# Squares from rows read back in the expert stage, one routing for three batches, the gate chain in the second phase, six banks for the first transposes

## The chip, the cores and the metric

The kernel runs on one NeuronCore of a Trainium2 chip. The metric is device time in microseconds, the median of several executions. The engines are TensorE (PE in the profile; PEld is its weight load), VectorE (DVE), ScalarE (ACT), GpSimd (POOL) and SyncE (SP, which here only issues DMAs). Each engine works through its own queue in order; an instruction that waits for another engine holds everything behind it on its own queue.

## What is computed

Causal attention with a decay per position, then a mixture of experts in which each token goes to its one best expert, then a dense layer with a maximum over three products.

```python
def _moe_ref(x, expert_emb, tau, w1, w2):
    xn = x / (np.linalg.norm(x, axis=-1, keepdims=True) + 1e-06)
    en = expert_emb / (np.linalg.norm(expert_emb, axis=-1, keepdims=True) + 1e-06)
    logits = xn @ en.T / tau
    expert_idx = np.argmax(logits, axis=1)
    probs = softmax(logits)
    gate_w = probs[np.arange(N), expert_idx]
    for e in range(E):
        mask = expert_idx == e
        out[mask] = gate_w[mask, None] * (np.maximum(x[mask] @ w1[e], 0.0) @ w2[e])

def reference(...):
    x = attention(q, k, v, f)            # 4 batches, 8 heads, 576 positions, 64 wide
    x = x as 2304 rows of 512
    x = _moe_ref(x, ...)                 # 8 experts, 512 -> 1024 -> 512
    h = max(x @ w1, x @ w2, x @ w3)      # 512 -> 768
    return h @ w_out                     # 768 -> 512
```

The norm of a row of x is not needed to choose the expert, only for the gate. The gate scales whole rows, and all products in between allow a positive scale to be pulled out, so the kernel multiplies by it once, at the very end.

## The kernel before

**Three parts.** `attention` (from L215) works through 4 batches x 8 heads, two heads (a pair) at a time. `moe` (from L911) first runs the eight experts, largest first, with a fixed capacity (`CAP`, 384 down to 256 tokens), and then the dense layer over six chunks of 384 tokens; I call these the expert stage and the second phase. Matrix products of weights are done as three matmuls, high x high, high x low, low x high (`mm3`, L906 to L908).

**Order.** Nothing is scheduled by hand. In both parts every step is a task for a small planner (`Sched`, L122 to L205) that runs while the program is built. A task has an engine or a choice of two, a cost in us, a due time (`prio`), tasks it depends on, and a buffer that it takes (`get`) or frees (`rel`). The planner always takes the task that can start first on its own clock, and among equals the one with the smallest due time, and emits it. So costs and due times fix the order of each engine's queue; on the chip the queues then run with semaphores. A `chain` is a generator whose steps are tasks that follow one another.

**Attention.** For each head: scores in pieces (`s`, L344, PE), the row minimum with the mask (L361, DVE), exp (L381, ACT), transposes (L393 to L401, PE), copies of these (L433 on DVE, L435 on ACT). For each pair, in two halves: `po` (L459, PE), a copy `ot`, `pb` (L478, PE; it turns the result back and appends its product with the expert rows), and a scaling into `XL` (L487, DVE). `po` and `pb` share two PSUM banks, `ps_o` (tag "o"). Splits of q and k into high and low part are casts on ACT or DVE (`evict`, L431 to L435) and subtractions on GpSimd (L321, L324). The rows of x go to DRAM (`x_dram`, L498) from SP's queue.

**At the end of a batch** (`batch_out`, L502) two chains start: `route_batch` (L567) finds the expert of each token of the batch's five blocks, its rank within the expert (PE sums over one-hot matrices), and adds the token numbers to a table (`route_table`, L680); `square_sums` (L699) takes five ACT squares with a running sum for the norms. The last batch goes through `first_slot` (L626), which finds the tokens of the largest expert at once. Chains of successive batches follow one another.

**Hand-over.** `sort_experts` (L735) puts the experts in order. `tokens` (L1054) gathers the rows of an expert's tokens in up to three groups (GpSimd, L1065), transposes each (PE, L1072, into an "o" bank) and splits it into high and low part (L934, L1083).

**Expert stage.** `expert_piece` loads a quarter of a weight matrix (SP, `stg`, three buffers), splits it (L934 and L951) into one of four `ring` slots. `ph` is x times w1, `py` h times w2; both use six PSUM banks (tag "y"). `Y` holds the results of all experts side by side; its part past the first expert is cleared by ACT (`clear`, L1103), since experts overlap there. `shared_piece` decodes the weights of the dense layer, which come as float64, with five DVE steps for each half (L1005 to L1020): eight of the twelve during the expert stage, the other four (the last of `w`, three of `w_out`) after the last expert's weights.

**side_work** (L880) computes the gates (`gates`, L795, with a square root and an exponential on ACT) and the table of output rows (`scatter_table`, L834, with PE sums of four times five matmuls), which gives `sidx` and `sgate`. It is queued with due time 30, after `sort_experts`.

**Second phase.** For each chunk: a split of Y (`ysplit`, L1199), 18 groups `pm` of twelve matmuls with the maximum on DVE (L1240), a split of the result (`g`), and three `po` (L1266 to L1268). ACT scales each `po` by `sgate` (`oo`, L1272) and GpSimd scatters it to the output (L1275).

Of the kernel before, what the change touches and what calls it, by code (L numbers as in the profile page):

```python
# [6 lines left out]
F32 = mybir.dt.float32  # L7
# [14 lines left out]
NBLK = 5  # L22
# [10 lines left out]
NCH = 3  # L33
# [181 lines left out]
def attention(tc, g, qT, kT, v, x_dram, es):  # L215
# [308 lines left out]
def routing_consts(nc, g, cp):  # L524
# [33 lines left out]
    g.ss = cp.tile([128, NTB], F32, name="ss")  # L558
    g.oh = cp.tile([128, NTB, E], F16, name="oh")
# [7 lines left out]
def route_batch(nc, g, b, lg, rp, ps):  # L567
    s0 = NBLK * b
    sl = slice(s0, s0 + NBLK)
    SH, SC = [128, NBLK, E], [128, NBLK, NCH]  # L570
    last = b == B - 1
    step = dict(eng="DVE", cost=0.24)
    yield dict(eng="DVE", cost=0.45)
    L = g.L[:, sl, :]
    nc.vector.tensor_reduce(out=L, in_=lg().rearrange("p t h c -> p t c h"), op=ALU.add, axis=AX.X)
    yield step
    mx = g.lmax[:, sl]
    nc.vector.tensor_reduce(out=mx, in_=L, op=ALU.max, axis=AX.X)
    yield step
    e1 = rp.tile(SH, F32, tag="e1", name="e1")  # L580
    nc.vector.tensor_tensor(out=e1, in0=L, in1=mx.unsqueeze(2).to_broadcast(SH), op=ALU.is_equal)
    yield step
    nc.vector.tensor_tensor(out=e1, in0=e1, in1=g.w8, op=ALU.mult)
    yield step
    e2 = rp.tile([128, NBLK], F32, tag="e2", name="e2")
# [5 lines left out]
    yield dict(eng="PE", cost=0.2, get=("o", ("pr", b)))  # L591
    pr = ps.tile([128, 512], F32, tag="o", name=f"pr{b}")
    w = NBLK * E
    fl = oh.rearrange("p t e -> p (t e)")
    nc.tensor.matmul(pr[:, 0:w], g.tris, fl, start=True, stop=False)
    if b:
        nc.tensor.matmul(pr[:, 0:w].rearrange("p (t e) -> p t e", e=E), g.ones,
                         g.ohs.unsqueeze(1).to_broadcast(SH), start=False, stop=False)
    for d in range(1, NBLK):
        nc.tensor.matmul(pr[:, d * E:w], g.ones, fl[:, 0:w - d * E], start=False, stop=(d == NBLK - 1))  # L600
# [3 lines left out]
    yield dict(eng="DVE", cost=0.24, rel=[("o", ("pr", b))])  # L604
    r1 = rp.tile(SH, F32, tag="r1", name="r1")
# [6 lines left out]
    rm, rq = positions(nc, ri, NBLK, rp, "rb")  # L612
    yield dict(eng="DVE", cost=0.8)
    ohp = onehot_pos(nc, g, rm, NBLK, rp, "rb")
    yield step
    rc = rp.tile(SC, F32, tag="rc", name="rc")
    nc.vector.tensor_tensor(out=rc, in0=g.ioc, in1=rq.unsqueeze(2).to_broadcast(SC), op=ALU.is_equal)
    yield from route_table(nc, g, b, ohp, rc, rp, ps)
# [60 lines left out]

def route_table(nc, g, b, ohp, rc, rp, ps):  # L680
    sl = slice(NBLK * b, NBLK * b + NBLK)
    oh = g.oh[:, sl, :]
    SC, SR = [128, NBLK, NCH], [128, NBLK, E, NCH]
    step = dict(eng="DVE", cost=0.24)
    yield step
    nc.vector.tensor_tensor(out=rc, in0=rc, in1=g.idv[:, b, :].unsqueeze(2).to_broadcast(SC), op=ALU.mult)
    yield step
    rr = rp.tile(SR, F16, tag="rr", name="rr")
    nc.vector.tensor_tensor(out=rr, in0=oh.unsqueeze(3).to_broadcast(SR), in1=rc.unsqueeze(2).to_broadcast(SR), op=ALU.mult)
    yield dict(eng="PE", cost=0.2, get=("o", ("pt", b)))  # L690
    pt = ps.tile([128, 512], F32, tag="o", name=f"ptab{b}")
    for t in range(NBLK):
        nc.tensor.matmul(pt[:, 0:E * NCH], ohp[:, t, :], rr[:, t].rearrange("p e c -> p (e c)"),
                         start=(t == 0), stop=(t == NBLK - 1))
    yield dict(eng="DVE", cost=0.24, rel=[("o", ("pt", b))])
    nc.vector.tensor_tensor(out=g.tab, in0=g.tab, in1=pt[:, 0:E * NCH].rearrange("p (e c) -> p e c", c=NCH), op=ALU.add)
# [214 lines left out]
def moe(tc, g, x_dram, w1, w2, m2, mo, out, rp, es):  # L911
# [142 lines left out]
    def tokens(k, use, before, deps=()):  # L1054
        done = []
        for c in range(NCH):
# [36 lines left out]
    sd.chain(side_work(nc, g, g.cp, rp, ps_o), 30.0, [sorted_])  # L1093
# [366 lines left out]
```

## Time and profile before

| | us |
|---|---|
| median of 3 runs | 785.78 |
| lowest and highest | 785.52, 785.88 |
| the profiled execution | 785.06 |
| its span in the profile | 783.3 |

| engine | busy us | share of the span |
|---|---|---|
| PE | 738.9 | 94% |
| DVE | 461.9 | 59% |
| ACT | 368.2 | 47% |
| POOL | 237.7 | 30% |

The span runs from the first to the last instruction of one execution. Busy time adds up the time in which an engine has at least one instruction under way; matmuls are pipelined, so short gaps between them don't show. A row of the timeline gives the start in us, the duration in us, engine, line, operation, written and read tiles, and in brackets the idle time of the engine just before it with what ended it. PEclk is the granted TensorE clock, 1.00 for 2.4 GHz and 0.50 for 1.2 GHz.

### The profile page before, as it was taken

To read this page: it belongs to the slowest core of one execution; us is meant where nothing else is said; L and a number is where in the kernel's file an instruction comes from. 1 tells how busy PE (TensorE), PEld (TensorE's weight loads), DVE (VectorE), ACT (ScalarE), POOL (GpSimd) and SP (SyncE) were. 2 spreads that over 40 slices of the span, in tenths; PEclk is the share of its full clock that TensorE was granted. 3 is DMA by queue.
4 is the path that set the end of the run, shared out by engine and by line. 5 is a ranking of instruction groups with operands and counts; after the bars stand their busy time and mean duration, and the time that the engine had idled before them with its cause. 6 is when DMAs were issued, how large, how long until landed. Compare 5 with 4: busy or idle time off the path is not lost.

```text
span 783.3 us, 13403 instructions
## 1 busy us (share of the span) xinstructions
PE 738.9 (94%) x4862; PEld 682.3 (87%) x4862; DVE 461.9 (59%) x1076; ACT 368.2 (47%) x870; POOL 237.7 (30%) x189
## 2 busy tenths in 40 slices
PE   2989999999949998999999999999999999999996
PEld 1868877778738998999999999989999899999995
DVE  6888887988567998867767877941211211112110
ACT  5668887978836653454554563231211212212111
POOL 7464443532020344234223113341221211212112
PEclk9999999999978999999999999999999999999998
DMA  9959775751145465556474653200000000100001
GB/s 228 239 125 216 191 178 143 182 118 40 23 116 208 151 220 181 186 181 233 151 257 147 230 198 126 82 28 14 1 40 1 28 14 1 41 0 15 28 1 43
DMA packets 44614, 90.19 MB, mean 115 GB/s; under 512 B 23320, under 2 KB 23320, under 8 KB 44544
## 3 DMA queue, kind: packets, MB, share of 16 engines
q1 hardware_dynamic: 40960, 77.83, 34.0%
q0 software_dynamic: 3152, 9.88, 3.5%
q10 hardware_dynamic: 432, 1.57, 0.5%
q8 instruction: 40, 0.66, 0.3%
q14 instruction: 30, 0.25, 0.1%
HBM read 74.97 MB, written 9.44 MB: 108 GB/s over the span
## 4 chain that ended last, share of the span: by engine, by line
PE 75%; DVE 9%; DMA 7%; issue 4%; ACT 1%; POOL 1%; SPq 1%; POOLq 0%; DVEq 0%; ACTq 0%
PE pm L907 10%; PE pm L906 10%; PE pm L908 10%; PE s L344 6%; PE po L459 6%; PE t L397 4%; PE ph L908 3%; PE ph L907 3%; PE py L906 3%; PE py L908 3%; PE ph L906 3%; PE py L907 3%; PE po L1268 3%; PE po L1267 3%; PE po L1266 3%
## 5 line engine op out<-in xcount | busy, mean ns | idle before, releaser
L1240 DVE TENSOR_TENSOR tm<-pm,tm 128x384 f32<-128x384 f32 x72 | 40.1, 557 | 199.4 <-PE pm L908 198.2
L907 PE MATMUL pm<-x_y,m 128*128 128x384 f32 x432 | 144.5, 335 | 0.0
L908 PE MATMUL pm<-x_y,m 128*128 128x384 f32 x432 | 144.4, 334 | 0.0
L906 PE MATMUL pm<-x_y,m 128*128 128x384 f32 x432 | 144.4, 334 | 0.0
L381 ACT ACTIVATE P<-P,nm 128x576 f32<-128x576 f32 (+4 forms) x160 | 88.3, 555 | 17.0 <-DVE nm L361 16.7
L344 PE MATMUL s<-R,At 128*128 128x192 f32 (+1 forms) x192 | 71.3, 380 | 14.9 <-DVE At L271 10.5
L934 ACT ACTIVATE w<-stg 128x1024 fp32r<-128x1024 f32 x63 | 66.2, 1056 | 33.3 <-DMA stg<-in_w_dram 14.4
L907 PEld LDWEIGHTS pm<-x_y,m 128*128 128x128 f32 x432 | 81.1, 188 | 0.6 <-POOL x_y L1199 0.3
L951 DVE TENSOR_TENSOR w<-stg,w 128x1024 fp32r<-128x1024 f32 x54 | 70.2, 1304 | 19.3 <-ACT w L934 18.9
L907 PE MATMUL ph<-x,w 128*128 128x384 f32 (+7 forms) x256 | 79.3, 310 | 2.1 <-DVE x L1083 2.1
L906 PEld LDWEIGHTS pm<-x_y,m 128*128 128x128 f32 x432 | 81.1, 188 | 0.2
L908 PEld LDWEIGHTS pm<-x_y,m 128*128 128x128 f32 x432 | 81.1, 188 | 0.0
L906 PE MATMUL py<-h,w 128*128 128x384 f32 (+7 forms) x256 | 79.5, 311 | 0.8 <-DVE h L1141 0.8
L908 PE MATMUL ph<-x,w 128*128 128x384 f32 (+7 forms) x256 | 79.4, 310 | 0.8 <-DVE w L951 0.7
L906 PE MATMUL ph<-x,w 128*128 128x384 f32 (+7 forms) x256 | 79.4, 310 | 0.7 <-ACT x L934 0.7
L1251 POOL TENSOR_TENSOR g<-tm,g 128x384 fp32r<-128x384 f32 x34 | 36.5, 1074 | 141.4 <-ACT g L934 141.4
L908 PE MATMUL py<-h,w 128*128 128x384 f32 (+7 forms) x256 | 78.5, 307 | 0.4 <-DVE w L951 0.4
L907 PE MATMUL py<-h,w 128*128 128x384 f32 (+7 forms) x256 | 78.2, 305 | 0.0
L934 ACT ACTIVATE g<-tm 128x384 fp32r<-128x384 f32 x36 | 18.8, 524 | 115.9 <-DVE tm L1240 115.9
L361 DVE CUSTOM_DVE_ANT_0 P<-s,mask 128x288 f32<-128x288 f32 (+4 forms) x160 | 64.4, 422 | 11.1 <-PE s L344 6.7
L344 PE MATMUL s<-R,Bt 66*128 66x192 f32 (+1 forms) x192 | 60.2, 320 | 4.3 <-DMA R<-clo 4.3
L321 POOL TENSOR_TENSOR At<-q,At 64x1152 fp32r<-64x1152 f32 x15 | 40.3, 2684 | 77.1 <-DVE At L433 24.7
(246 smaller groups left out, 1620.4 us busy)
## 6 DMA issues: line engine op xcount, KB each, us to landing
stg<-in_w_dram SPq DMA_DIRECT2D x61, 512.0 KB
q<-in_q_dram SPq DMA_DIRECT2D x32, 288.0 KB
k<-in_k_dram SPq DMA_DIRECT2D x32, 288.0 KB
sd<-in_m_dram SPq DMA_DIRECT2D x18, 512.0 KB
Bt<-At SPq DMA_DIRECT2D x16, 288.0 KB
v<-in_v_dram SPq DMA_DIRECT2D x4, 1024.0 KB
x_dram<-XL SPq DMA_DIRECT2D x64, 64.0 KB
sd_o<-in_mo_dram SPq DMA_DIRECT2D x6, 512.0 KB
```

The lines of the kernel that those rows point to most:

```text
L321: nc.gpsimd.tensor_tensor(out=At[i][64:128], in0=raws[p][0][64:128], in1=At[i][64:128].bitcast(F32), op=ALU.subtract)
L344: nc.tensor.matmul(st[:, 0:wp], lt[0:kk, r, ROW0[t]:ROW0[t] + 128], rt[0:kk, r, j0:j0 + wp], start=(ps_i == 0), stop=(ps_i == 1))
L361: nc.vector.tensor_tensor_reduce(out=P[0:n, j0:j0 + w], in0=st_.pop((h, t, k))[0:n, 0:w], in1=g.mask[0:n, m0:m0 + w], scale=-0.125, scalar ...
L381: nc.scalar.activation(out=P[0:n, 0:ext], in_=P[0:n, 0:ext], func=AF.Exp, bias=nm[0:n, k:k + 1], scale=-1.0, accum_out=sums[b][0:n, t, h % ...
L459: nc.tensor.matmul(po[64 * r:64 * r + 64, lo - c0:w], vt[b][0:n, a, (2 * hp + r) * D:(2 * hp + r + 1) * D], PT[(2 * p + r) % NPT][0:n, a, ...
L906: nc.tensor.matmul(out, whi, xhi, start=start, stop=False)
L907: nc.tensor.matmul(out, whi, xlo, start=False, stop=False)
L908: nc.tensor.matmul(out, wlo, xhi, start=False, stop=stop)
L934: nc.scalar.activation(out=out, in_=in_, func=AF.Copy)
L951: ENG[e].tensor_tensor(out=w[:, 1], in0=t, in1=w[:, 0].bitcast(F32), op=ALU.subtract)
L1240: nc.vector.tensor_tensor(out=mx[0], in0=mx["p", w][:, 0:MC], in1=mx[0], op=ALU.max)
L1251: ENG[e].tensor_tensor(out=ht[:, 1, :], in0=mx[0], in1=ht[:, 0, :].bitcast(F32), op=ALU.subtract)
```

## The change

Four things change.

Only the last batch takes its squares during attention. For batches 0 to 2 the rows of x are read back from `x_dram` in the expert stage: four loads on SP's queue into the still unused part of `Y` (three of 128 x 4 x 512 floats for the blocks of 128 rows, one of 64 x 3 x 512 for the short blocks), and 15 ACT squares there, each before that part of `Y` is cleared. `ss` is set to 1.0 first.

Batches 0 and 1 only store their logits (`logits`). At the end of batch 2 one routing handles the 15 blocks of batches 0 to 2: the same steps on three times the width, then three rounds of comparison (`onehot_pos`) and five matmuls into one bank, and one addition to the table.

`side_work` starts after the last expert's `ph` and the squares, with due time now + 8 at the end of the expert stage, and the scaling of each `po` waits for its end.

The three transposes of the first expert's tokens go to the six "y" banks instead of the two "o" banks.

```diff
@@ batch_out
-        sd.chain(g.square_sums(b, lambda: XL[b][:, :, :, 0:D]), pr + 40, deps + [consts_done])
+        if b == B - 1:
+            sd.chain(g.square_sums(b, lambda: XL[b][:, :, :, 0:D]), pr + 40, deps + [consts_done])
@@ routing_consts
+    nc.vector.memset(g.ss, 1.0)
@@ route_batch
+def logits(nc, g, b, lg):
+    yield dict(eng="DVE", cost=0.75)
+    nc.vector.tensor_reduce(out=g.L[:, NBLK * b:NBLK * b + NBLK, :], in_=lg().rearrange("p t h c -> p t c h"), op=ALU.add, axis=AX.X)
+def route_batch(nc, g, b, lg, rp, sp, ps):
+    yield from logits(nc, g, b, lg)
+    if b < B - 2:
+        return
     last = b == B - 1
+    m, b0 = (1, b) if last else (B - 1, 0)
+    s0, nb = NBLK * b0, NBLK * m
...
+    yield from row_ids(nc, g, oh, b0, m, rc, rr)
+    for c in range(m):
+        yield dict(eng="DVE", cost=0.83)
+        ohp = onehot_pos(nc, g, rm[:, NBLK * c:NBLK * c + NBLK], NBLK, keep, "rb")
+        yield dict(eng="PE", cost=0.2, get=None if c else ("o", ("pt", b)))
+        if c == 0:
+            pt = ps.tile([128, 512], F32, tag="o", name=f"ptab{b}")
+        table_sums(nc, pt, ohp, rr[:, NBLK * c:NBLK * c + NBLK], c == 0, c == m - 1)
+    yield dict(eng="DVE", cost=0.24, rel=[("o", ("pt", b))])
+    table_add(nc, g, pt)
@@ tokens
-                pt = gat[k, c] = ps_o.tile([128, 512], F32, tag="o", name=f"xt{k}_{c}")
+                pt = gat[k, c] = (ps_o if k else ps_h).tile([128, 512], F32, tag="o" if k else "y", name=f"xt{k}_{c}")
@@ moe
     sorted_ = sd.chain(sort_experts(nc, g, g.cp, rp, ps_o), 6.0)
-    sd.chain(side_work(nc, g, g.cp, rp, ps_o), 30.0, [sorted_])
...
-    zero = [sd.task("ACT", 1.8, lambda e, d=d: clear(e, d), now + 16, [wsplit[1, 0, 3]]) for d in range(KC)]
+    def fetch(e, d):
+        if d < B - 1:
+            nc.sync.dma_start(out=room[d], in_=xv[d, 64:S].rearrange("(t p) d -> p t d", p=128))
+        else:
+            nc.sync.dma_start(out=room[d][0:64, 0:B - 1], in_=xv[0:B - 1, 0:64].rearrange("b p d -> p b d"))
+    def square(e, d, i):
+        n, col = (128, NBLK * d + 1 + i) if d < B - 1 else (64, NBLK * i)
+        x = room[d][0:n, i]
+        nc.scalar.activation(out=x, in_=x, func=AF.Square, accum_out=g.ss[0:n, col:col + 1])
+    zero, norms = [], []
+    for d in range(KC):
+        xl = sd.task("SP", 1.5, lambda e, d=d: fetch(e, d), now + 10 + 5 * d, [wsplit[1, 0, 3]], lat=4.0)
+        mine = [sd.task("ACT", 0.62, lambda e, d=d, i=i: square(e, d, i), now + 18 + 6 * d, [xl]) for i in range(4 if d < B - 1 else B - 1)]
+        zero.append(sd.task("ACT", 1.8, lambda e, d=d: clear(e, d), now + 18 + 6 * d, mine))
+        norms += mine
...
+    side = sd.chain(side_work(nc, g, g.cp, rp, ps_o), now + 8, [sorted_] + norms + hlast[-1:])
...
-            te = sd.task("ACT", act(DM), oev, now, [pe_], get=("scr", ("o", col)), rel=[("y", ("o", col))])
+            te = sd.task("ACT", act(DM), oev, now, [pe_, side], get=("scr", ("o", col)), rel=[("y", ("o", col))])
```

## Rows read from the trace of the kernel before

**Rows 1.** Windows, attention: us, busy (instructions) per engine, PEclk, DMA share, GB/s

```profile
118.74:130.57 11.83, 11.83 (x98) 9.59 (x100) 9.87 (x37) 9.91 (x32) 4.32 (x3) 1.00 0.58 138
80.97:118.74 37.77, 36.09 (x300) 29.31 (x302) 32.80 (x116) 31.51 (x103) 16.94 (x7) 1.00 0.78 186
130.57:168.38 37.81, 36.09 (x302) 29.34 (x303) 32.81 (x116) 31.51 (x103) 16.96 (x7) 1.00 0.73 174
180.21:220.95 40.74, 40.74 (x355) 32.70 (x355) 25.26 (x103) 30.72 (x101) 2.24 (x1) 1.00 0.14 30
```

**Rows 2.** Timeline of DVE and PE, some 15 us after batch 0's end

```profile
101.89 3.07 DVE L433 CAST R<-k 128x1152 fp32r<-128x1152 f32 x1
105.16 0.41 PE L344 MATMUL s<-R,At 128*128 128x320 f32 x1 [0.84 <-DVE nm L361]
```

**Rows 3.** Timeline of PE, expert stage: first matmuls, then three waits

```profile
239.11 0.52 PE L908 MATMUL ph<-x,w 128*128 128x384 f32 x1
241.99 0.47 PE L908 MATMUL ph<-x,w 128*128 128x384 f32 x1
275.75 0.43 PE L907 MATMUL ph<-x,w 128*128 128x352 f32 x1 [0.39 <-DVE x L1083]
295.56 0.43 PE L906 MATMUL py<-h,w 128*128 128x352 f32 x1 [0.85 <-DVE h L1141]
311.66 0.42 PE L907 MATMUL ph<-x,w 128*128 128x336 f32 x1 [1.68 <-DVE x L1083]
```

**Rows 4.** Windows, expert stage to second phase; columns as in rows 1

```profile
240.00:280.00 40.00, 39.61 (x235) 38.98 (x235) 33.67 (x69) 25.59 (x34) 9.97 (x6) 0.97 0.55 191
236.00:240.00 4.00, 3.15 (x9) 2.38 (x10) 2.34 (x7) 2.72 (x3) 0.94 (x1) 0.50 0.64 212
465.00:480.00 15.00, 15.00 (x118) 14.69 (x117) 9.19 (x13) 7.30 (x13) 3.39 (x4) 1.00 0.43 148
480.00:515.00 35.00, 35.00 (x202) 34.93 (x202) 33.66 (x47) 9.11 (x18) 13.06 (x11) 1.00 0.21 76
```

**Rows 5.** Timeline of DVE, routing at the end of batch 0

```profile
85.49 0.76 DVE L575 TENSOR_REDUCE L<-XL 128x40 f32<-128x320 f32 x1
88.95 0.82 DVE L724 TENSOR_TENSOR ohp<-iota,rm 128x640 f16<-128x640 f32 x1
91.87 0.17 DVE L623 TENSOR_TENSOR ohs<-ohs,o 128x8 f16<-128x8 f16 x1
```

**Rows 6.** Line view, squares: count, ns min/median/max, first and last start, form

```profile
L703 ACT ACTIVATE sq<-XL x20: 615/624/630, 85.8 to 224.6; 128x512 f32<-128x512 f32 x20
```

**Rows 7.** Timeline of the hand-over, GpSimd and PE

```profile
230.82 0.95 POOL L1065 DMA_INDIRECT gat<-x_dram,gidx  x1 [0.30 <-issue]
236.12 1.09 PE L1072 MATMUL xt<-ident,gat 128*128 128x128 f32 x4 [1.85 <-DVE ov L783]
```

**Rows 8.** View of the gather tile, 225 to 240 us

```profile
DMA to landing us min/median/max: 3.6/3.8/4.1
```

**Rows 9.** Timeline of DVE, expert stage: side chain, and one decode step

```profile
238.55 0.17 DVE L799 TENSOR_SCALAR nrm<-ss 128x20 f32<-128x20 f32 x1
261.38 3.03 DVE L724 TENSOR_TENSOR ohp<-iota,rm 128x640 f16<-128x640 f32 x1
302.09 0.18 DVE L876 TENSOR_SCALAR ctidx<-a 128x18 uint32<-128x18 f32 x1
307.40 3.07 DVE L1009 SCALAR_TENSOR_TENSOR dec<-sd,dec 128x512 int32<-128x512 int32 x1
```

**Rows 10.** Waits of PE, expert stage: us in total, times, longest us

```profile
PE ph L908 <- DVE w L951: 0.7, 1, 0.7
```

**Rows 11.** Timeline of DVE and PE, first chunk of the second phase

```profile
512.63 0.69 DVE L1020 SCALAR_TENSOR_TENSOR sd_o<-sd_o,dec_o 128x512 f32<-128x512 int32 x1
514.87 0.39 PE L1266 MATMUL po<-m_o,g 128*128 128x512 f32 x1
516.56 2.99 DVE L1199 TENSOR_TENSOR x_y<-Y,x_y 128x384 fp32r<-128x384 f32 x3
```

More of the change, by code (lines that the diff above doesn't have):

```diff
@@ L590, in route_batch @@
                                    op1=ALU.is_equal)
-    yield dict(eng="PE", cost=0.2, get=("o", ("pr", b)))
+    yield dict(eng="PE", cost=0.05 * (nb + 1), get=("o", ("pr", b)))
     pr = ps.tile([128, 512], F32, tag="o", name=f"pr{b}")
-    w = NBLK * E
+    w = nb * E
     fl = oh.rearrange("p t e -> p (t e)")
     nc.tensor.matmul(pr[:, 0:w], g.tris, fl, start=True, stop=False)
-    if b:
+    if b0:
         nc.tensor.matmul(pr[:, 0:w].rearrange("p (t e) -> p t e", e=E), g.ones,
                          g.ohs.unsqueeze(1).to_broadcast(SH), start=False, stop=False)
-    for d in range(1, NBLK):
-        nc.tensor.matmul(pr[:, d * E:w], g.ones, fl[:, 0:w - d * E], start=False, stop=(d == NBLK - 1))
+    for d in range(1, nb):
+        nc.tensor.matmul(pr[:, d * E:w], g.ones, fl[:, 0:w - d * E], start=False, stop=(d == nb - 1))
     if last:
@@ L603, in route_batch @@
         return
-    yield dict(eng="DVE", cost=0.24, rel=[("o", ("pr", b))])
-    r1 = rp.tile(SH, F32, tag="r1", name="r1")
+    yield dict(eng="DVE", cost=0.3, rel=[("o", ("pr", b))])
     nc.vector.tensor_tensor(out=r1, in0=pr[:, 0:w].rearrange("p (t e) -> p t e", e=E), in1=oh, op=ALU.mult)
@@ L677, in first_slot, with row_ids, table_sums, table_add @@
     g.rest = ohp, rc
-def route_table(nc, g, b, ohp, rc, rp, ps):
[L681 to L689, printed above, removed]
+def row_ids(nc, g, oh, b0, m, rc, rr):
+    nb = NBLK * m
+    SC, SR = [128, nb, NCH], [128, nb, E, NCH]
+    yield dict(eng="DVE", cost=0.24)
+    idv = g.idv[:, b0:b0 + m, :].rearrange("p b t -> p (b t)")
+    nc.vector.tensor_tensor(out=rc, in0=rc, in1=idv.unsqueeze(2).to_broadcast(SC), op=ALU.mult)
+    yield dict(eng="DVE", cost=0.28 * m)
+    nc.vector.tensor_tensor(out=rr, in0=oh.unsqueeze(3).to_broadcast(SR), in1=rc.unsqueeze(2).to_broadcast(SR), op=ALU.mult)
+def table_sums(nc, pt, ohp, rr, first, last):
+    for t in range(NBLK):
+        nc.tensor.matmul(pt[:, 0:E * NCH], ohp[:, t, :], rr[:, t].rearrange("p e c -> p (e c)"),
+                         start=(first and t == 0), stop=(last and t == NBLK - 1))
+def table_add(nc, g, pt):
+    nc.vector.tensor_tensor(out=g.tab, in0=g.tab, in1=pt[:, 0:E * NCH].rearrange("p (e c) -> p e c", c=NCH), op=ALU.add)
+def route_table(nc, g, b, ohp, rc, rp, ps):
+    oh = g.oh[:, NBLK * b:NBLK * b + NBLK, :]
+    rr = rp.tile([128, NBLK, E, NCH], F16, tag="rr", name="rr")
+    yield from row_ids(nc, g, oh, b, 1, rc, rr)
     yield dict(eng="PE", cost=0.2, get=("o", ("pt", b)))
     pt = ps.tile([128, 512], F32, tag="o", name=f"ptab{b}")
-    for t in range(NBLK):
-        nc.tensor.matmul(pt[:, 0:E * NCH], ohp[:, t, :], rr[:, t].rearrange("p e c -> p (e c)"),
-                         start=(t == 0), stop=(t == NBLK - 1))
+    table_sums(nc, pt, ohp, rr, True, True)
     yield dict(eng="DVE", cost=0.24, rel=[("o", ("pt", b))])
-    nc.vector.tensor_tensor(out=g.tab, in0=g.tab, in1=pt[:, 0:E * NCH].rearrange("p (e c) -> p e c", c=NCH), op=ALU.add)
+    table_add(nc, g, pt)
 def square_sums(nc, g, b, x, rp):
```

42 lines of the change are left out of this document (22 added, 20 removed).

## The prediction

> **What bounds the kernel now.** I read the page's busy table first: TensorE (PE) is busy nearly always, VectorE (DVE) and ScalarE (ACT) much less. An average over three stages says little, so next came the windows, stage by stage, and then, inside each stage, the waits of PE and the order of the instructions. In each the reader is to see which engine PE waits for, and what that engine was doing just before.
>
> Attention (0 to 221 us): four head pairs to a batch. An undisturbed pair takes 11.83 us; the three pairs that follow the end of batch 0 take 37.77 us and those after batch 1 37.81 us, against 3 x 11.83 = 35.49 [rows 1]. In these stretches PE idles 1.7 us (36.09 busy), and in the others shown not at all. One such wait is 0.84 us for a row minimum of DVE, which was held by a cast of 3.07 us [rows 2].
> Hand-over (221 to 238 us): a chain over DVE, a gather and transposes, with PE mostly idle.
> Experts (238 to 477 us): PE dense; three waits for DVE stand out, 0.39, 0.85 and 1.68 us [rows 3].
> Second phase (477 to 783 us): PE dense. DVE is full only in its first 35 us (33.66 of 35), decoding the last four shared weights [rows 4].
>
> **Attention, part by part.** A batch end now costs DVE 17 routing instructions (first, longest and last in the rows, 4.5 us together) [rows 5] and ACT five squares of 0.62 us, 3.1 us and the reads of the sums on top [rows 6]. After the change batches 0 and 1 keep only the first instruction, 0.76 us, and no squares. I put the whole excess on this work: in the three pairs DVE is busy 32.80 us against 3 x 9.87 = 29.6 for undisturbed ones, ACT 31.51 against 3 x 9.91 = 29.7 [rows 1]. So 37.77 - 35.49 = 2.28 and 37.81 - 35.49 = 2.32, together **-4.6 us**. Bounds: 0 (the planner writes another order, with waits of its own) and -4.6.
> Batch 2 gets one routing for 15 blocks: its 17 instructions become 19, three of them the 0.82 us comparison, one the 0.76 us sum, the other 15 with up to three times the elements; between the rows of 0.17 us (8 results from 8 elements) and 0.76 us (320 elements) I put one at 0.3 us, an estimate near the small end because most have 120 elements or fewer: 0.76 + 2.46 + 4.5 = 7.7 us against 4.5. The squares give ACT back 3.1 us and more. In this stretch DVE is busy 25.26 and ACT 30.72 of 40.74 us [rows 1], so the room is there: **0**, bounds -1.5 and +1.5. Two new waits lie here. The one-hot tile has one buffer, so the second and third comparison wait on DVE for PE's sums, and row minima queue behind them. The table holds one of two "o" banks for three rounds, which `po` and `pb` share; PE has score and transpose work of later heads meanwhile. The new memset of `ss` is one small DVE instruction: nothing.
>
> **Hand-over.** The third group of transposes starts at 236.12, released by DVE's L783, though its gather was issued at 230.82 and gathers land after 3.6 to 4.1 us, median 3.8 [rows 7, 8]. With a bank of its own it starts at 230.82 + 3.8 = 234.62: **-1.5 us** (bounds -1.2 and -1.7, by 4.1 and 3.6). The two copies behind it, on ACT and DVE, just move up; next late would be the second weight piece, and PE needs that only after 24 matmuls.
>
> **Experts, what leaves.** `side_work`, gates and scatter table, stands on DVE from 238.55 to 302.09, 59 instructions, 21.9 us (first and last in the rows) [rows 9]. The first two waits come right behind its instructions: -1.24 us. The third waits for a split that stands behind a decode step of 3.07 us [rows 9]: it belongs to the DVE's load but not to the chain, so I count half, -0.84. **-2.1 us**. A wait of 0.7 us for a weight's split late in the stage [rows 10] may go too, or stay; I leave it. The chain's 20 scatter matmuls only move: 0.
>
> **Experts, what comes.** Four read-backs on SP's queue, 3 x 1.05 + 0.39 = 3.5 MB. The DMA engines are 0.55 busy at 191 GB/s between 240 and 280 us [rows 4], so 3.5 MB cost 3.5 MB / (191 GB/s / 0.55) = 10 us of them, out of 18 idle. Weight loads queue behind them on SP, three buffers ahead of PE. Then 15 squares on ACT, 15 x 0.62 = 9.4 us and their reads, and the four clears of Y, which stay but wait for the squares, and expert 1's write of Y for them. ACT is busy 25.59 of the 40 us from 240, clears included [rows 4], so 9.4 us and the reads fit into the 14.4 left, and the side chain's square root, exponential and table loads leave. ReLUs and weight copies may wait up to a square or a clear; PE has six banks to run ahead. I take 0; the dear end is one more wait like the longest now, +1.7. Bounds of the stage: -1.24 - 1.68 - 0.7 = -3.6, and +1.7.
>
> **Second phase.** The side chain starts at expert 7's last `ph`, about 465 us. From there to 515 us DVE is idle 5.8 + 1.3 us [rows 4]. The chain's due time (now + 8) lies ahead of the late weights' (now + 20 and later), so wherever both are ready the planner takes the chain, and decoding gets only its pauses. Decoding ends now at 512.63 + 0.69 = 513.3, and the first `po`, which needs w_out, starts at 514.87 [rows 11]: no slack. With 21.9 us more and 7.1 us of room it ends near 513.3 + 21.9 - 7.1 = 528.1. The planner knows that w_out is late; it can run the next chunk's `pm` first. These need the next split of Y, now hidden under `po`: its last DVE part ends at 516.56 + 2.99 = 519.55 [rows 11]. Uncovered, PE gets the fourth quarter of its operand at 519.55 instead of 514.87 plus nine matmuls at 0.17 us (35.00 us / 202 [rows 4]) = 516.4: **+3.1 us**. Bounds: 0 (the chain fits into pauses) and 528.1 - 514.9 = +13.2 (PE stands until w_out is there). The planner's costs decide for the first, since `pm` becomes ready long before. The new wait on ACT (the first `oo` for the chain's end) has later ACT copies behind it, but three `po` and the next `pm` fit the six banks: 0.
> PE's granted clock was 0.50, the 1.2 GHz level, in 236 to 240 us, after the broken work of the hand-over [rows 4]. A matmul of 384 columns steps 0.32 us there (239.11 to 241.99, nine steps in 2.88 us) [rows 3] and 0.17 at full clock. The Trainium skill, TensorE: Matmul & The Clock Gate, Part 1: The HAM clock gate, says that an idle array falls back to the half rate and sustained activity releases it; the trace agrees at the hand-over. Here the pauses come in pieces of about 1 us, between matmuls, so I add nothing and keep the fall as a rival.
>
> **Sum.** -4.6 + 0 - 1.5 - 2.1 + 0 + 3.1 = -5.1 us. On the profiled execution 785.06 - 5.1 = 780.0 us (its span is 783.3, 1.8 us lies around it); on the median 785.78, which is 0.7 above that execution, **780.7 us**.
>
> **The rivals.**
> The chain is hidden: its pauses, with DVE's idle 7 us, let w_out be decoded in time; -8.2, 777.6 us. For it speak the chain's own pauses (two steps on ACT, four turns through PE), against it DVE's 33.66 of 35.
> Attention gives nothing: the order written for batches 1 to 3 is a new one, and casts slowed to 3 us meet row minima elsewhere; -1.5 - 2.1 + 3.1 = -0.5, 785.3 us. For it speaks that the waits stand 15 us after the routing.
> **Slower: PE waits for w_out.** The first `po` is put before the next `pm`, in order, and PE stands from 514.9 to 528.1. -4.6 - 1.5 - 2.1 + 13.2 = +5.0, 790.8 us; slower than before from a wait of 8.2 us on. For it speaks that DVE decodes slower than planned when GpSimd runs beside it (3.03 us for the comparison that takes 0.82 alone [rows 5, 9]).
> The clock falls at the uncovered split: twelve steps at 0.32 instead of 0.17 us, as many as at the start of the stage, +1.8 on the forecast, 782.5 us.
> The change doesn't do what it says in the expert stage: read-back and squares bring as much waiting as the chain took, +1.7 instead of -2.1: 784.5 us.
>
> **How the numbers follow.** Forecast 0.42, chain hidden 0.16, no gain in attention 0.17, PE waits for w_out 0.13, clock 0.06, expert stage 0.06. Differences under 0.2% (1.6 us) can't be told from no change here. Faster: 0.42 + 0.16 + 0.06 = 0.64; same: 0.17 + 0.06 = 0.23; slower: 0.13. The range reaches from the hidden chain with the cheap ends of batch 2 and the expert stage, 777.6 - 1.5 - (3.6 - 2.1) = 774.6, to no gain in attention with two dear ends, 785.3 + 1.5 + 1.7 = 788.5. It leaves out the full wait for w_out (0.13) and little else.
>
> **What would show it.** Right: the three pairs after each batch end near 35.5 us; third transposes about 1.5 us after the second; no PE wait for DVE before 300 us; DVE full from 465 to about 528 us; `pm` of the second chunk ahead of the first `po`. Wrong: PE waits on squares, clears or weights between 250 and 300 us, or a PE gap over 8 us before the first `po`.

## The result, and the profile after

The changed kernel takes 796.31 us (median; 795.9 to 798.4) where the kernel before takes 785.83 beside it: a ratio of 1.0144, with an interval of 1.0122 to 1.0167. It is slower by 10.5 us; 780.7 us, 5 us faster, was predicted, and the range ended at 788.5. The profiled execution of the changed kernel took 795.97 us, its span is 794.2.

Four marks in the trace cut the span into stages: the first `po` of the attention's second head pair (53.63 us before, 53.62 after), `pr` (the rank sums that open the hand-over), the first `ph` and the first `pm`. The last column runs from the first `pm` to the first `po` of the second chunk and holds the opening of the second phase; what follows takes 218.6 us in both kernels.

| us | second pair's `po` to `pr` | `pr` to first `ph` | first `ph` to first `pm` | opening |
|---|---|---|---|---|
| before | 170.28 | 13.99 | 239.16 | 87.66 |
| after | 166.90 | 13.23 | 242.58 | 99.20 |
| difference | -3.4 | -0.8 | +3.4 | +11.5 |

So the attention paid, the expert stage gave back as much, and the opening of the second phase lost more than the whole result. Windows of the attention after (us; busy and instructions of PE, PEld, DVE, ACT, POOL; PEclk; DMA share; GB/s): an undisturbed pair, the three pairs after batch 0 and after batch 1, and the stretch after batch 2, which answer to [rows 1].

```profile
116.38:128.25 11.87, 11.87 (x98) 9.62 (x97) 9.56 (x36) 9.97 (x32) 5.48 (x3) 1.00 0.64 151
80.93:116.38 35.45, 35.45 (x289) 28.94 (x288) 27.13 (x100) 29.56 (x95) 15.59 (x7) 1.00 0.83 194
128.25:163.70 35.45, 35.45 (x289) 28.93 (x288) 27.14 (x100) 29.55 (x95) 15.58 (x7) 1.00 0.77 186
175.57:217.50 41.93, 41.91 (x374) 33.47 (x374) 27.10 (x104) 28.14 (x92) 2.31 (x1) 1.00 0.13 29
```

PE now has no gap in the three pairs: 35.45 us busy of 35.45, where they took 37.77 and 37.81. Of the 2.3 us in each, 1.7 were PE's waits and 0.6 its own matmuls, the rank and table sums of the routing. After batch 2 those come back: 41.91 us busy with 374 instructions, where it was 40.74 with 355.

The hand-over, GpSimd's third gather and the transposes that it releases ([rows 7, 8]):

```profile
227.43 0.95 POOL L1099 DMA_INDIRECT gat<-x_dram,gidx  x1 [0.31 <-issue]
231.95 1.11 PE L1106 MATMUL xt<-ident,gat 128*128 128x128 f32 x4 [1.17 <-DMA gat<-x_dram,gidx]
```

The expert stage, PE's waits from 236 to 476 us (us in total, times, longest), which answer to [rows 3, 10]:

```profile
PE py L942 <- DVE w L985: 2.8, 4, 1.1
PE ph L942 <- DVE w L985: 1.6, 3, 0.8
PE ph L942 <- POOL w L985: 0.9, 1, 0.9
PE py L940 <- ACT w L968: 0.7, 1, 0.7
```

The three early waits for the side chain and what stood behind it are gone; in their place PE waits 6.0 us for weights, all of it after 405 us. How such a wait comes about is seen in the timeline around the longest (start, us, engine, line, operation):

```profile
396.14 0.34 SPq L1033 DMA_DIRECT2D sd<-in_m_dram  x1
396.72 5.20 SPq L998 DMA_DIRECT2D stg<-in_w_dram  x3
402.92 0.42 DVE L1039 TENSOR_SCALAR dec<-sd 128x512 int32<-128x512 int32 x1
407.03 0.69 DVE L1054 SCALAR_TENSOR_TENSOR sd<-sd,dec 128x512 f32<-128x512 int32 x1
408.84 1.77 DVE L1064 TENSOR_TENSOR m<-sd,m 128x512 fp32r<-128x512 f32 x1
410.63 0.34 SPq L1033 DMA_DIRECT2D sd<-in_m_dram  x1
411.18 2.09 SPq L998 DMA_DIRECT2D stg<-in_w_dram  x3
416.43 1.06 ACT L968 ACTIVATE w<-stg 128x1024 fp32r<-128x1024 f32 x1 [5.73 <-DMA stg<-in_w_dram]
419.19 0.40 PE L942 MATMUL py<-h,w 128*128 128x288 f32 x1 [1.12 <-DVE w L985]
```

A shared load (`sd`) is issued at 396.14; its one buffer is free when decode and split are through, at 408.84 + 1.77 = 410.61; the next shared load goes at 410.63, and three expert weights (`stg`), which stand behind it in SP's queue, only then. They reach ScalarE at 416.43 and PE at 419.19. After that wait PE's clock fell too, to a mean of 0.60 in 420 to 424 us, which cost some 1.6 us (0.40 of 4).

The opening of the second phase, first its timeline, then two windows (columns as above); they answer to [rows 11] and [rows 4]:

```profile
515.27 0.34 PE L942 MATMUL pm<-x_y,m 128*128 128x384 f32 x1
518.07 0.69 DVE L1054 SCALAR_TENSOR_TENSOR sd_o<-sd_o,dec_o 128x512 f32<-128x512 int32 x1
518.79 0.66 ACT L968 ACTIVATE m_o<-sd_o 128x512 fp32r<-128x512 f32 x1 [3.65 <-DVE sd_o L1054]
519.36 1.75 ACT L968 ACTIVATE x_y<-Y 128x384 fp32r<-128x384 f32 x4
519.53 1.29 POOL L1064 TENSOR_TENSOR m_o<-sd_o,m_o 128x512 fp32r<-128x512 f32 x1 [2.38 <-ACT m_o L968]
519.92 0.69 PE L940 MATMUL pm<-x_y,m 128*128 128x384 f32 x1 [4.31 <-ACT x_y L968]
520.78 5.24 POOL L1252 TENSOR_TENSOR x_y<-Y,x_y 128x384 fp32r<-128x384 f32 x4
530.35 0.69 DVE L1054 SCALAR_TENSOR_TENSOR sd_o<-sd_o,dec_o 128x512 f32<-128x512 int32 x1
532.02 0.39 PE L1319 MATMUL po<-m_o,g 128*128 128x512 f32 x1
```

```profile
480.00:515.00 35.00, 35.00 (x217) 34.37 (x216) 33.88 (x62) 7.89 (x16) 10.48 (x8) 1.00 0.18 61
515.00:532.00 17.00, 11.02 (x40) 8.96 (x39) 16.16 (x23) 4.09 (x9) 10.12 (x9) 0.70 0.09 32
```

As forecast, 36 `pm` of chunk 1 come ahead of the first `po`, and their split of Y is uncovered. But the split's copies stand on ACT behind the copy of a w_out piece (518.79) that waits for DVE's decode; on GpSimd the low parts stand behind that piece's low part, and end at 520.78 + 5.24 = 526.02. From the last `pm` of chunk 0 to the first `po`, with the 36 between, pass 532.02 - 515.27 = 16.75 us; at 0.173 us a matmul these 37 steps would take 6.4. Another 1.3 us of the opening is the chain's 20 scatter matmuls, which left the expert stage: the 216 `pm` of chunk 0 take 39.1 us with them and took 37.8 without.

### The profile page after: what moved, and what is told of

It reads as the page before. It is cut to its first block, busy times and chain, and to the rows that moved or that the text cites. A ratio compares the mean times of both kernels' runs of the same rounds, so it can differ in the third digit from the quotient of the medians.

```text
span 794.2 us, 13361 instructions
## 1 busy us (share of the span) xinstructions
PE 744.6 (94%) x4860; PEld 685.5 (86%) x4860; DVE 452.3 (57%) x1055; ACT 368.2 (46%) x871; POOL 213.6 (27%) x180
## 4 chain that ended last, share of the span: by engine, by line
PE 83%; DVE 7%; DMA 3%; issue 3%; ACT 1%; POOL 1%; SPq 0%; POOLq 0%; DVEq 0%; ACTq 0%
PE pm L941 9%; PE pm L942 9%; PE pm L940 9%; PE s L344 7%; PE po L459 6%; PE t L397 5%; PE ph L942 4%; PE ph L940 4%; PE ph L941 4%; PE py L942 4%; PE py L940 4%; PE py L941 4%; PE po L1320 3%; PE po L1321 3%; PE po L1319 3%
## 5 line engine op out<-in xcount | busy, mean ns | idle before, releaser
L940 PE MATMUL pm<-x_y,m 128*128 128x384 f32 x432 | 146.2, 338 | 4.3 <-ACT x_y L968 4.3
L941 PE MATMUL pm<-x_y,m 128*128 128x384 f32 x432 | 146.4, 339 | 1.7 <-POOL x_y L1252 1.5
L942 PE MATMUL pm<-x_y,m 128*128 128x384 f32 x432 | 145.6, 337 | 0.0
L985 DVE TENSOR_TENSOR w<-stg,w 128x1024 fp32r<-128x1024 f32 x61 | 76.2, 1251 | 27.7 <-ACT w L968 27.1
L940 PEld LDWEIGHTS pm<-x_y,m 128*128 128x128 f32 x432 | 82.1, 190 | 4.8 <-ACT x_y L968 4.6
L941 PEld LDWEIGHTS pm<-x_y,m 128*128 128x128 f32 x432 | 81.9, 190 | 4.1 <-POOL x_y L1252 3.4
L942 PE MATMUL py<-h,w 128*128 128x384 f32 (+7 forms) x256 | 79.5, 311 | 2.8 <-DVE w L985 2.8
L942 PEld LDWEIGHTS pm<-x_y,m 128*128 128x128 f32 x432 | 82.0, 190 | 0.0
L940 PE MATMUL py<-h,w 128*128 128x384 f32 (+7 forms) x256 | 80.2, 313 | 0.7 <-ACT w L968 0.7
L941 PE MATMUL py<-h,w 128*128 128x384 f32 (+7 forms) x256 | 79.0, 309 | 0.0
L968 ACT ACTIVATE g<-tm 128x384 fp32r<-128x384 f32 x36 | 18.8, 523 | 114.3 <-DVE tm L1293 114.3
```

The costliest lines, as they stand in the source:

```text
L940: nc.tensor.matmul(out, whi, xhi, start=start, stop=False)
L941: nc.tensor.matmul(out, whi, xlo, start=False, stop=False)
L942: nc.tensor.matmul(out, wlo, xhi, start=False, stop=stop)
L968: nc.scalar.activation(out=out, in_=in_, func=AF.Copy)
L985: ENG[e].tensor_tensor(out=w[:, 1], in0=t, in1=w[:, 0].bitcast(F32), op=ALU.subtract)
```

## Experiments

**Where the chain stands.** One run moves the chain back to its old due time (it starts when the squares are summed), one lets the decode of w_out go first.

```diff
+    side = sd.chain(side_work(nc, g, g.cp, rp, ps_o), 30.0, [sorted_] + norms)
...
-    side = sd.chain(side_work(nc, g, g.cp, rp, ps_o), now + 8, [sorted_] + norms + hlast[-1:])
```

```diff
-    side = sd.chain(side_work(nc, g, g.cp, rp, ps_o), now + 8, [sorted_] + norms + hlast[-1:])
+    side = sd.chain(side_work(nc, g, g.cp, rp, ps_o), now + 40, [sorted_] + norms + hlast[-1:])
```

> The whole changed kernel, but the gate and table chain has its old due time and starts as soon as the squares are summed, early in the expert stage. Theory A (the chain's 26 us on VectorE after 466 us make the decode of w_out late, the last decode step ending near 531 us, and the planner then puts 36 matmuls of the next chunk ahead of the first product with w_out): the second phase is as in the kernel before, the first po comes right behind chunk 0's last pm, and about 10.5 of the 11.6 us lost there come back: 784 to 788 us. Rival B (w_out comes late through the loads and the late expert stage, whatever VectorE does): the order of po and pm stays as in the changed kernel and the time stays at 793 to 797 us.

> The changed kernel with one number changed: the chain in the second phase is due 32 us later, behind the last shared pieces, so that VectorE decodes w_out first and the chain fills what is left. Theory A: w_out is ready before chunk 0's last pm, po comes ahead of the next chunk's pm again, the split of Y lies beside it, and the first outputs wait for the end of the chain near 531 us in spare PSUM banks: 785 to 788 us. Rival E (54 us of VectorE work between 477 and 531 us are too much in whatever order; the outputs wait for the chain and TensorE for their banks): 792 to 797 us.

With the chain early the opening takes 87.61 us, as in the kernel before: theory A holds for that stage. The whole does not gain: 798.72 us, ratio to the kernel before 1.0181 (1.0143 to 1.0219), since the expert stage now takes 250.84 us. PE's waits there:

```profile
PE py L940 <- DVE h L1194: 7.0, 2, 5.5
PE py L942 <- DVE w L985: 2.2, 4, 1.2
PE py L940 <- ACT w L968: 1.5, 1, 1.5
```

In the kernel before the chain ran from 238.55 to 302.09 [rows 9]; behind the read-back it starts at 278.5, and expert 2's ReLU splits (the last row) stand behind its steps on DVE (two of these in the first rows):

```profile
288.61 2.22 DVE L765 TENSOR_TENSOR mr<-perm,caps 128x64 f32<-128x64 f32 x1
296.19 3.13 DVE L884 TENSOR_TENSOR cc<-cc,valid 128x90 f16<-128x90 f16 x1
299.90 1.38 DVE L1194 SCALAR_TENSOR_TENSOR h<-ph,h 128x352 fp32r<-128x352 f32 x3
```

With the decode first: 796.69 us (ratio 1.0144, 1.0097 to 1.019), opening 98.56 us. Theory A's cure fails and rival E holds: `po` does come ahead of `pm`, but PE now stands for the chain's scatter matmuls in its own queue, and behind that its granted clock is 0.50 in 520 to 525 us:

```profile
PE ctps L893 <- DVE rr L887: 6.5, 2, 5.8
```

Two orders on DVE give the same stage within 0.7 us. So it is the sum of the work, chain and decode, that DVE can't do in 477 to 531 us, and the order only chooses what is late; with the chain elsewhere (the run above) the stage was as before.

**The clock.** 26 unused matmuls fill PE's gap:

```diff
...
+                for i in range(26):
+                    nc.tensor.matmul(pf[:, 0:MC], weight[0, 0][:, 0, 0:128], weight[0, 0][:, 0, 0:MC], start=True, stop=True)
```

> The changed kernel with 26 matmuls of 384 columns that compute nothing that is used, on TensorE behind chunk 0's last pm, where it stood still for 4.3 us and the granted clock then fell to 0.50. Theory J (the low parts of Y on GpSimd, the last at 526.0 us, hold chunk 1's first group anyway, and the clock only adds behind them): the clock stays at 1.00, first po 1 to 2 us earlier than 532.0, time 794 to 795.5 us. Rival K (the half clock, some 22 matmuls at 0.32 and not 0.17 us, is worth all it takes): first po 3 to 4 us earlier, 792 to 793.5 us.

Windows of this run, and GpSimd's low parts:

```profile
516.00:520.00 4.00, 3.61 (x20) 3.16 (x19) 3.90 (x10) 1.97 (x5) 1.61 (x2) 1.00 0.35 127
520.00:524.00 4.00, 1.59 (x6) 0.95 (x6) 3.93 (x5) 0.35 (x1) 4.00 (x4) 1.00 0.02 4
524.00:528.00 4.00, 3.83 (x13) 3.50 (x14) 3.93 (x5) 0.70 (x1) 2.58 (x3) 0.58 0.00 0
```

```profile
520.03 5.24 POOL L1252 TENSOR_TENSOR x_y<-Y,x_y 128x384 fp32r<-128x384 f32 x4
```

The clock stays at 1.00 until 524 us (after it was 0.50 in 520 to 528), and PE gains 0.33 us from first `pm` to first `po` (55.36 for 55.69): PE merely waits longer for the low parts, 3.0 us in three waits. 796.72 us, ratio 1.0152 (1.0116 to 1.0188). Theory J holds, with less than it gave; rival K falls.

**The read-back.** The four loads and 15 squares are left out (the norms stand at 1).

```diff
-        xl = sd.task("SP", 1.5, lambda e, d=d: fetch(e, d), now + 10 + 5 * d, [wsplit[1, 0, 3]], lat=4.0)
-        mine = [sd.task("ACT", 0.62, lambda e, d=d, i=i: square(e, d, i), now + 18 + 6 * d, [xl]) for i in range(4 if d < B - 1 else B - 1)]
+        mine = [wsplit[1, 0, 3]]
```

> The changed kernel without the four loads of x back and without their 15 squares (the norms of batches 0 to 2 are left out and stand at 1, so their gates are others); the clearing of Y and the chain in the second phase stay. Theory C (the four loads of 3.5 MB at 237 to 250 us, ahead of the weights in SP's queue, took the lead that the weights had; the first shared load was issued at 249.6 us instead of 240.8): the shared load is issued near 238 us, the n-th weight copy on ScalarE comes 3 to 8 us earlier through the stage, TensorE's 6.0 us of waits for weight splits between 405 and 460 us fall under 2 us, and the expert stage loses 3 to 5 us: 791 to 793.5 us. Rival D (the weights come at a pace of their own, set by the one buffer of the shared loads, whatever goes ahead of them): the waits for weight splits stay at 4 us or more and the time at 795 to 797 us.

Theory C falls. The shared loads start earlier (236.0 us), as expected, but the stage takes 242.50 us, and 794.82 us in all (ratio 1.0141, 1.0094 to 1.0189). Read-back and squares cost nothing that can be seen.

Four runs with the same or nearly the same order of the expert stage (after, and the runs with the decode first, with the filler and without the read-back) start it at 233.75, 236.34, 234.20 and 232.70 us, and first `pm` comes at 476.33, 476.51, 475.52 and 475.20: a start that varies by 3.6 us, an end by 1.3. It looked as if something other than PE set the end, and theory P below starts from that. The four stages, each in one window in this order, say something else:

```profile
233.75:476.33 242.58, 236.63 (x1616) 233.00 (x1617) 175.61 (x268) 134.76 (x227) 39.17 (x31) 0.98 0.60 207
236.34:476.51 240.17, 234.07 (x1616) 230.60 (x1617) 174.99 (x265) 134.96 (x227) 39.41 (x31) 0.99 0.61 209
234.20:475.52 241.32, 235.43 (x1617) 231.97 (x1617) 175.62 (x268) 135.02 (x227) 39.37 (x31) 0.99 0.61 208
232.70:475.20 242.50, 236.74 (x1617) 232.90 (x1617) 172.16 (x261) 127.12 (x200) 47.84 (x35) 0.98 0.57 192
```

PE idles 5.95, 6.10, 5.89 and 5.76 us, whatever the start: a late start does not shorten its waits. What differs is its busy time for the same matmuls, and that is the clock. One such place, behind two waits of nearly the same size (0.67 and 1.12 us after, 0.70 and 1.10 with the decode first), after and with the decode first:

```profile
420.00:424.00 4.00, 4.00 (x22) 4.00 (x21) 1.39 (x1) 1.30 (x4) 0.31 (x1) 0.60 0.59 167
420.00:424.00 4.00, 2.91 (x22) 2.92 (x23) 2.73 (x2) 2.79 (x5) 1.51 (x1) 1.00 0.19 58
```

**The pace of the weights.** First the 16 shared loads go to GpSimd's queue; then only SP's order is changed, each shared piece planned with one expert and each of its loads behind a given weight.

```diff
-                nc.sync.dma_start(out=t, in_=src[:, 1024 * h:1024 * h + 1024])
+                (nc.gpsimd if early else nc.sync).dma_start(out=t, in_=src[:, 1024 * h:1024 * h + 1024])
...
```

```diff
+    HOLD = [4, 10, 13, 18, 21, 24, 27, 30, 33, 37, 40, 44, 47, 50, 54, 57]
...
+            behind = [wloads[HOLD[2 * mkeys.index(key) + h]]] if early else []
...
```

> The changed kernel with the 16 shared loads of the expert stage issued from GpSimd's queue and not from SP's. Theory F (SP's queue is in order, and a shared load that waits for its one buffer, 71 us of waits between 300 and 450 us, holds back the weight loads behind it; that paces the weights late in the expert stage): SP's waits for that buffer are gone, weight copies come earlier, TensorE's waits for weight splits between 405 and 460 us go from 6.0 us to under 2 us: 790 to 793.5 us. Rival G (three weight buffers and the DMA engines pace the weights, and the shared buffer only takes slack): within 1 us of the changed kernel, 795 to 797 us, or slower if GpSimd's loads come late for the decode.

> The changed kernel; only the order of SP's queue in the expert stage is another: each of the 16 shared loads stands behind 44, 47, 51, 54 and 57 expert weights (from the twelfth on) where it stood behind 41, 44, 47, 51 and 54. Theory H (a shared load waits for its one buffer, some 12 to 15 us after the last, and the weights behind it wait with it; in the changed kernel the weights are one load less ahead of it than in the kernel before, so that the sixth expert starves): TensorE's 6.0 us of waits for weight splits between 405 and 460 us fall under 2 us, the stretch from the first ph to the first pm, 242.6 us in the changed kernel, becomes 237 to 239.5, and the time 791 to 793.5 us. Rival G (the weights have a pace of their own, three buffers and the landing of 512 KB, whatever stands between them): waits and time within 1 us of the changed kernel.

On GpSimd's queue it gets worse: 809.66 us (1.0273 to 1.0354), stage 252.67 us. SP no longer waits for the shared buffer, but the decode steps in DVE's queue wait for their loads, and weight splits stand behind them:

```profile
DVE dec L1039 <- DMA sd<-in_m_dram: 34.1, 14, 4.8
```

So theory F fails as a cure: the turn of the one buffer is as long as before, and its wait goes to whichever queue has something behind it. This run alone can't tell F from G. With the order of SP's queue changed the stage takes 239.87 us, PE waits 4.3 us for splits where it waited 6.0, its clock is 1.00 in 420 to 424 us, and the median is 794.31 us (ratio 1.0115, 1.0075 to 1.0154): less than theory H gave, more than rival G. The order counts, and is not all.

Next the turn itself: two buffers of half the size in the same memory and 32 loads of 256 KB, each with its own decode and split; packed ahead, as the planner orders them, and in a second run spread evenly by the table in the last line.

```diff
-                                        pool("std", 1), pool("m2p", 1))
+                                        pool("std", 2), pool("m2p", 1))
...
-        for h in range(2):
+        parts = 4 if early else 2
+        W = 1024 // parts
+        for h in range(parts):
```

```diff
+    HOLD = [4, 5, 7, 9, 10, 12, 14, 15, 17, 19, 21, 22, 24, 26, 27, 29, 31, 33, 34, 36, 38, 39, 41, 43, 45, 46, 48, 50, 51, 53, 55, 57]
```

> The changed kernel; the shared loads of the expert stage are cut in quarters (256 KB, 32 of them) with two buffers in the place of one of twice the size, so that a load need not wait for the decode of the one before. They run ahead: the last stands behind 40 weights in SP's queue and not 54. Theory P (the one shared buffer, 12 to 15 us a turn, gives the pace to the weights behind it in SP's queue, and that pace, not TensorE, sets the first pm at 475 to 476.5 us in every run whose first ph was at 232.7 to 236.3): late in the stage no weight stands behind a shared load, TensorE's 6.0 us of waits for splits between 405 and 460 us are under 1.5 us, first ph to first pm takes 235 to 239 us; 789 to 793 us. Rival G (three weight buffers, landing and splits have a pace of their own): the late waits stay at 4 us or more, 240 to 243 us, 795 to 797 us. Rival Q (32 loads packed early starve the first experts): waits move to 270 to 400 us and the stage is 243 us or more.

> The same quarters with two buffers, but spread evenly in SP's queue, one behind every 1.7 weights, the last behind 56. Theory P: less waiting at each shared load, 236 to 239.5 us from first ph to first pm, 790 to 793 us, if two buffers are enough; Rival G: 240 to 243 us and 795 to 797 us.

Packed ahead, the stage takes 242.00 us and the kernel 797.74 (two executions, 794.98 and 800.50), where rival G put them. Within the stage experts 7 and 8, behind the last shared load, run in 25.2 and 23.5 us (26.7 and 25.9 in the changed kernel), as theory P says, but expert 4 takes 33.4 us for 29.6: a loss in an early expert, as in rival Q, though PE waits there 2.2 us for a split of x and not for a weight. Spread, the stage takes **235.22 us** and the kernel 790.45 (1.0072, 1.0039 to 1.0105). The stage in one window (the changed kernel's stands above):

```profile
234.34:469.56 235.22, 233.42 (x1616) 230.96 (x1617) 181.21 (x346) 137.35 (x243) 52.59 (x49) 0.99 0.66 213
```

PE idles 235.22 - 233.42 = 1.8 us where it idled 5.95. Theory P's cure holds, with more than it gave (236 to 239.5 us): nothing but the shared loads and their decode was touched, and 7.4 us came back, 4.2 of waiting and 3.2 of busy time at a higher clock. Neither half of it does that alone: quarters packed ahead gave 242.00 us, halves held back 239.87.

**Attention and hand-over.** One routing and six banks, the squares left in the attention, the chain early and without a read-back.

> The kernel before with one routing for batches 0 to 2 and the six banks for the first transposes, but with all squares still in the attention on ScalarE and the chain in its old place early in the expert stage; x isn't read back. Theory L (in the attention half of the gain is VectorE's routing and half ScalarE's squares): batches 0 and 1 give 2 to 3 us, the hand-over 0.75, the expert stage and the second phase stay as before: 782 to 784 us on this chip's scale with the kernel before at 785. Rival M (ScalarE's squares alone bound the pair): nothing from the attention, 784.5 to 786 us. Rival N (what is gained ahead of the expert stage is given back to the weights' pace): first ph earlier, but first pm within 1 us of the kernel before, 784.5 to 786 us.

From the second pair's `po` to `pr` takes 166.87 us, the whole of the gain, with all squares on ACT in the attention: 170.28 in the two kernels that route each batch by itself (before, and before with quarters), 166.9 in ten others with one routing for three batches, 167.5 in the run with the chain early. Theories L and M fall: **the gain was the routing's alone**, and moving the squares added nothing to it. The total, 789.69 us (1.0038 to 1.0081), is slower than before: its expert stage takes 245.63 us, for the planner wrote another order (expert 2 took 39.6 us, 34.6 in the kernel before). Rival N is right that the gain does not reach the end; the loss is more than it gave, and most of it lies in expert 2, not late in the stage. Hand-over: 13.06 us here, but 13.23 to 14.40 in the others with six banks, against 13.99 and 14.22 without.

**A version that uses this.** The chain behind the fourth expert, first with the halves held back, then with spread quarters (in both the first four steps of the second phase's first group are also kept in order); and the spread quarters on the kernel before.

```diff
+        if k == 3:
+            side = sd.chain(side_work(nc, g, g.cp, rp, ps_o), total, [sorted_] + norms + h_pe[-1:])
...
```

> The order of SP's queue as in the run with the shared loads held back, and the gate and table chain spread behind the fourth expert (due with the end of the stage) and not in the second phase. Theory A with slack: VectorE is busy some 21 of 28 to 30 us there, so the chain's 26 us fit beside it in three to four experts, the opening of the second phase is as in the kernel before (37.8 us from the first pm to the first po), and with theory H the expert stage stays near 239 to 241 us: 780 to 785 us. Rival I (anywhere in the expert stage the chain delays weight splits and hidden parts on VectorE, as where it stood early: 250.8 us against 242.6): the opening of the second phase is mended, but the expert stage is 246 to 251 us and the time 789 to 795 us.

> Spread quarters with two buffers, and the gate and table chain behind the fourth expert and not in the second phase. Theory A and theory P: the opening of the second phase takes 37.8 us from first pm to first po, the expert stage 237 to 242 us with the chain's 26 us on VectorE beside it; 780 to 785 us. Rival I (the chain delays splits on VectorE there, as where the halves were held back: 244.1 us): 244 to 247 us, 787 to 791 us.

> The kernel before with the shared loads in quarters and two buffers, spread as in the run before this one, nothing else. Theory P (in the kernel before TensorE was late by the half clock and the chain, so the pace of the weights hardly showed: 0.7 and 0.4 us of waits): 237 to 239.5 us from first ph to first pm where it took 239.2, 784 to 786 us. Rival G: 239 to 240 us, no difference. Rival R (more and shorter instructions on VectorE and ScalarE delay the splits): 240 us or more, 786.5 us or more.

With halves: opening mended (88.46 us), stage 244.14 us, between the two theories, and 789.67 us (1.0027 to 1.0064), in rival I's range. With quarters: stage 238.34, opening 87.68, **782.27 us, ratio 0.9968 (0.9948 to 0.9987)**, as theories A and P gave it and faster than both kernels, than the kernel before by 0.3%. Its windows:

```profile
480.00:515.00 35.00, 35.00 (x196) 33.81 (x195) 32.36 (x45) 11.21 (x22) 15.15 (x13) 1.00 0.18 61
515.00:532.00 17.00, 17.00 (x90) 15.83 (x89) 1.11 (x2) 2.89 (x5) 3.87 (x4) 1.00 0.12 46
```

DVE is through with the decode by 515 us and PE never stops. On the kernel before, spread quarters cost: 789.77 us (1.0044 to 1.0098), stage 243.67 us. There the chain stands on DVE up to 304.2 us, and PE waits early:

```profile
PE xt L1078 <- DVE x L1089: 3.0, 1, 3.0
PE ph L907 <- DVE x L1089: 1.8, 1, 1.8
PE py L906 <- DVE h L1146: 1.4, 1, 1.4
```

Expert 2 takes 41.3 us for 34.6, more than the whole loss. Rival R's range, open above, holds this; whether shorter instructions or the new order do it was not told apart.

## Why the prediction was wrong, by its own steps

- **Attention, -4.6: right for the pairs.** The three pairs lost 2.32 and 2.36 us; forecast 2.28 and 2.32. The cause was half wrong: I put the excess on DVE's routing and ACT's squares, but the squares had no part in it, and 0.6 us in each was PE's own sums. That the size came out is in part luck. Batch 2, forecast 0 with 1.5 either way, cost 1.2 us: these sums, for 15 blocks at once, which I counted on DVE only. Together -3.4, as much as PE's waits in the two stretches (1.68 and 1.72 us).
- **Hand-over, -1.5: too much.** The third transposes are now released by their own gather, as said, but it landed 4.5 us after its issue (227.43 to 231.95), outside the 3.6 to 4.1 of [rows 8]; 0.8 us in this run, and nothing steady over the others.
- **Experts, what leaves, -2.1: right in place, then lost. This step failed:** it carried a gain upstream to the stage's end and put new waits for weights at nothing. The early waits went and experts 1 to 4 took 4.4 us less (134.27 to 129.86 us; 1.3 of them the 20 scatter matmuls that moved). But waits for weight splits went from 1.1 us (0.7 of them in [rows 10]) to 6.0, and the clock fell behind two of them; experts 5 to 8 took 7.8 us more (104.89 to 112.72); net +3.4. That these waits come from the turn of the one shared buffer is shown: 4.3 us with the halves held back, 1.7 with spread quarters. The fall of the clock, some 1.6 us, is chance: two runs with nearly the same waits did not have it. Why the kernel before has so few of these waits is not shown. Its PE comes later, but the run with the chain early and the one with one routing and six banks, whose PE comes later still, wait 4.4 and 3.8 us for weights. The planner also put the last five shared loads one weight further back there: behind 45, 48, 51, 55 and 58 weight loads, behind 44, 47, 50, 54 and 57 in the changed kernel (counted by issues in the traces, of 64).
- **Experts, what comes, 0: right.** Without read-back and squares the stage is the same within 0.1 us.
- **Second phase, +3.1: right mechanism, mis-sized, and the largest error.** The order was right, and the end of the decode nearly (forecast 528.1, measured 531.04). **The failed step is the end of Y's split:** I took it from where it stands in the kernel before, 519.55 [rows 11]. There the decode was through, at 513.3, before the split began, and three of the four low parts ran on DVE. After, ACT and GpSimd hold w_out's copies ahead of it, which wait for the decode, all four low parts stand on GpSimd, and the last ends at 526.02, 6.5 us later. With matmuls at half clock behind that the stretch lost 10.3 us, and the opening 11.5 where 3.1 was forecast: 8.4 of the 15.6 us between forecast and result. My upper bound, +13.2, holds it.
- **The rivals.** "PE waits for w_out" (790.8) had the right sign by another wait: PE waits for a split whose engines wait for w_out. The clock fell, as its rival said, and it was worth 0.3 us and not 1.8, since GpSimd was later; it also fell in the expert stage, behind waits of about 1 us, a size for which I had added nothing. The range left out the dear end of the second phase, and no case joined it with a loss in the expert stage.

What stays open: why the orders that the planner writes for the expert stage differ by several us for small changes ahead of it. In the three runs with the chain early (whole change, one routing, quarters on the kernel before) expert 2 takes 40.1, 39.6 and 41.3 us; in the kernel before, with the chain early too, it takes 34.6. The planner orders the queues by its own times, and a queue once written stands for whatever is behind; which of the moved instructions does it was not followed up.

## What to carry to other kernels

When a bottleneck engine is almost gapless, find out how far its supplier is ahead before you bank a gain upstream; a supplier with a turn of its own (one buffer, load, decode, split, then the next load) can take the gain back, and the repair is in that turn. A stage that ends at nearly the same time in several runs is no proof of such a supplier: compare waits and busy time first, since the clock can make the ends agree. When work is moved into a stage where an engine is full, price not only that engine's end, but every queue in which something else stands behind the work that it makes late. Spread the moved work where the engine has room, and measure the stages one by one: here two gains and two losses hid in one number.

## What the runs showed that I had not expected

- An in-order queue hands on a wait rather than removing it: with the shared loads on GpSimd's queue the waits went from SP to DVE (34.1 us in 14 waits) and the kernel lost 13 us more.
- PE's clock fell to 0.50 after one wait of 4.31 us. After 0.67 and 1.12 us of waiting near 418 us it fell to a mean of 0.60 in 420 to 424, but after 0.70 and 1.10 us with the decode first it stayed at 1.00, and so it did after the single wait of 1.68 us in the kernel before [rows 3] (1.00 in 308 to 330 us). Keeping PE busy kept the clock at 1.00 up to 524 us, and bought 0.3 us where another engine was late anyway.
- A short DVE step can last as long as a GpSimd split beside it. With the chain early, the step of 64 elements at 288.61 took 2.22 us, its twin just ahead 0.27; the one of 90 elements took 3.13. Both end with one of these (GpSimd, same run; the first row is two splits, the first of them about half of it):

```profile
288.34 4.82 POOL L985 TENSOR_TENSOR w<-stg,w 128x1024 fp32r<-128x1024 f32 x2 [4.16 <-ACT w L968]
296.85 2.35 POOL L985 TENSOR_TENSOR w<-stg,w 128x1024 fp32r<-128x1024 f32 x1
```

- The second pair's first `po` comes at 51.9 to 56.1 us over the profiled runs, a spread larger than most of the differences sought. The first `po` of all comes at 33.1 to 35.6 us. From there 18.8 us pass in the runs whose mean granted clock in 30 to 56 us is 1.00, 20.3 where it is 0.93 and 21.3 to 21.9 where it is 0.87; near 48 us PE waits 2.4 us for a row minimum. So stages, not ends, must be compared.
